# Seven products for eight on every superblock, with a new slot and mirror policy and all ReLUs on ScalarE: a gated-attention and maxout kernel

## The chip, the cores and the metric

One core of one Trainium2 chip runs the whole kernel in one launch. The metric is the device time of one execution in microseconds (us). Engine names: PE is TensorE's matmuls and PEld its weight loads, DVE is VectorE, ACT is ScalarE, POOL is GpSimd, SP is SyncE, which in this kernel only issues DMAs: four loads at the start, and from then on transposes. A suffix q (SPq, ACTq) marks work of an engine's sequencer, such as issuing a DMA.

The kernel before took 947.47 us (median of 3 runs, 943.57 to 948.69).

## The reference

```
B, S, D, d_qk, d_ff = 8, 3072, 256, 64, 1024
scores = z @ z^T / S                     # per batch, S x S, symmetric
x = u * (relu(scores)**2 @ v)            # gated attention, S x D
out = maximum(x @ w1, x @ w2) @ w_out    # maxout feed-forward, d_ff wide
```

The kernel uses max(a, b) = relu(a - b) + b, so the feed-forward becomes `relu(x @ (w1 - w2)) @ w_out + x @ (w2 @ w_out)`.

## The kernel before

A batch's 3072 rows are six groups of 512, and two groups make a superblock, so there are three superblocks per batch (c = 0, 1, 2) and 24 "couples" (batch, superblock). The squared scores are kept as blocks of 512 x 512 in bf16 slots of SBUF. Because scores are symmetric, only blocks on or above the diagonal are computed. The block below is the *mirror*, made by a DMA transpose. On a diagonal block three *triangle* pieces are mirrored. SyncE also issues the *turns*: transposes of u (for the gate) and of z (for the next scores).

From batch 1 on, a couple's attention product is not done as eight quarter products but as seven (P1, P5, P6, P7, X11, X12, X21), for which VectorE makes block sums S1 to S4 and sums of v. Before, this was done for the two superblocks off the diagonal (`o != c`), while the superblock's own blocks went plainly (D22 and the own parts of the X products). A couple is then:

- a *product stage*: 88 steps of two half-array matmuls, with the score pairs of later couples between them;
- two *ffs* of the couple before, during which VectorE works off a task list: gates of the couple just finished, then S1, S2, S3 and the sums of v for the next.

```python
def score_pair(b, g, m, ...):              # two score tiles: matmul, ReLU, square
    ...
    def finish():
        nc.vector.tensor_mul(a[:, k : k + 2, :], r, r)          # square (cut)
        if triangle and k:
            for j in range(G - 1):                              # 3 triangle pieces
                nc.sync.dma_start_transpose(a[:, j + 1 :, ts(j, P)], a[:, j, (j + 1) * P :])
        if k and blk > g:
            ...
            to_mirror.append((b, g, blk))
            mirror_ready()

def mirror_ready(keep=0):
    while to_mirror and len(free) > keep:  # mirror as soon as a slot is free
        mirror(*to_mirror.pop(0))

def turn_u(b, g):
    t = upool.tile([P, G, KD, P], bf16, name="uT")
    nc.sync.dma_start_transpose(t.rearrange(...), un[b, g].rearrange(...))

def ff(b, g, xT, ...):
    for nb in range(KF):                   # KF = 8 tiles d_ps
        ...                                # two matmuls into d_ps
        if nb in (2, 5, 7):
            nc.vector.tensor_single_scalar(out=g_sb[:, nb, :], in_=d_ps, scalar=0.0, op=ALU.max)
        else:
            nc.scalar.activation(g_sb[:, nb, :], d_ps, AF.Relu)
        hook(1, nb)                        # one VectorE task, at some places
    for t0 in range(0, G, 2):
        ...                                # 20 matmuls into o_ps
        nc.scalar.copy(o_sb, o_ps)
        nc.scalar.dma_start(out=dst[:, ds(t0, 2), :], in_=o_sb)   # the store: ScalarE issues it

# main loop, one couple (much cut)
(42 if b else 6, lambda: turn_u(b, q1)),   # program steps at which u is turned
(48 if b else 14, lambda: turn_u(b, q2)),
...
return forms, list(gates) + sums[:3] + tasks + sums[3:]   # VectorE's list: the gates come first
```

VectorE works its list in order, and the gates, which read the turned u, stand at its head: in the trace of before, gates, sums and sums of v run in the order of the list in all 21 couples that have sums. And the DMAs issued by SyncE and by ScalarE share eight completion semaphores: in before as in after, their 415 DMAs use eight in one common rotation, and in none of the 407 cases with a predecessor on the same semaphore does an issue start before that one has landed (the earliest starts 0.06 us after it in before, 0.08 in after). So a store on ScalarE may have to wait for a transpose that stands eight DMAs before it in the program; in after such waits held ScalarE's next copy 7 times, 60.2 us in all.

## Time and profile before

| | before |
|---|---|
| median of 3 runs | 947.47 us |
| span of the profiled run | 943.4 us |
| PE / DVE / ACT busy | 99% / 76% / 59% |
| product stage, medians of superblock 0 / 1 / 2 | 21.80 / 21.48 / 22.12 us |
| first ff / second ff | 8.04 / 8.09 to 8.14 us |

The stage times here and below are worked out from the timeline, as differences of the starts of matmul groups (first product matmul, first `d_ps` matmul of each ff), as medians over batches 1 to 6.

From the page of the profile of before: the span, the busy time of each engine with its share and instruction count, PE's busy tenths in 40 equal slices, and the shares of the chain of waits.

```profile
span 943.4 us, 19492 instructions
...
PE 929.3 (99%) x7706; PEld 517.5 (55%) x7706; DVE 717.3 (76%) x1158; ACT 552.8 (59%) x1062; POOL 57.0 (6%) x111
...
PE   8997999999999999999999999999999999999998
...
PE 91%; DVE 5%; ACT 1%; issue 1%; DMA 1%; SPq 0%; ACTq 0%; DVEq 0%
```

PE works in nearly every slice, and the chain that ended last is 91% PE. So here time is won only by removing matmuls and lost only by making PE wait.

Groups of before (line, engine, operation, tiles, count | busy us, mean ns of one | idle before, and what ended most of it):

```profile
L829 PE MATMUL acc<-blk,v_sb 64*128 64x512 bf16 x2544 | 467.1, 376 | 0.0
...
L829 PE MATMUL acc<-blk,vt 64*128 64x512 bf16 x1344 | 328.6, 376 | 0.0
...
L432 ACT ACTIVATE g_sb<-d_ps 128x512 bf16<-128x512 f32 x240 | 130.3, 599 | 56.8 <-PE d_ps L420 52.3
...
L428 DVE TENSOR_SCALAR g_sb<-d_ps 128x512 bf16<-128x512 f32 x144 | 96.2, 685 | 42.6 <-PE d_ps L420 34.2
```

The two L829 groups are the product matmuls, 3888 in all. The ffs' ReLUs are shared: 240 on ACT, 144 on DVE.

Waits of before by engine (us in total, times, longest):

```profile
PE d_ps L420 <- ACT o_sb L456: 3.9, 1, 3.9
...
PEld L448 <- DVE g_sb L428: 7.0, 21, 0.5
...
ACT o_sb L456 <- DMA blk<-blk: 6.1, 1, 6.1
```

PE hardly waits.

ScalarE's timeline of before at the end of a first ff:

```profile
389.82 0.34 ACTq L457 DMA_DIRECT2D out_dram<-o_sb  x1
390.26 2.74 ACT L432 ACTIVATE g_sb<-d_ps 128x512 bf16<-128x512 f32 x5 [0.47 <-PE d_ps L420]
```

The store of the last output tile is issued at once (the copy before it had ended at 389.79), and the second ff's ReLUs follow 0.1 us later.

### The profile page before, as it was taken

What the parts mean: (1) busy time and instruction counts of PE and PEld (TensorE: products, weight loads), DVE (VectorE), ACT (ScalarE), POOL (GpSimd) and SP (SyncE); (2) the same over time, 40 slices, a digit from 0 to 9 for tenths busy, and PEclk for the clock granted to TensorE, in tenths of its full rate; (3) what the DMA queues carried; (4) which work ended last, traced back from release to release, by engine and by line L of the source; (5) the groups of instructions that cost most, each with busy time, mean ns of one, the idle gap of its engine ahead of it and who ended that gap; (6) DMA issues with size and microseconds to landing.
All of it is one profiled execution on the core that took longest, in us unless ns stands there. A gap on an engine that the chain in (4) does not pass through costs nothing.

```text
span 943.4 us, 19492 instructions
## 1 busy us (share of the span) xinstructions
PE 929.3 (99%) x7706; PEld 517.5 (55%) x7706; DVE 717.3 (76%) x1158; ACT 552.8 (59%) x1062; POOL 57.0 (6%) x111
## 2 busy tenths in 40 slices
PE   8997999999999999999999999999999999999998
PEld 4454465554555555555546555465465554655555
DVE  6772588778887787987878869788688787885651
ACT  6793856556556566566565565655756657563333
POOL 3100000000000000000000000000000000000000
PEclk9998999999999999999999999999999999999999
DMA  9999999989999995998979999799979889985301
GB/s 190 148 201 210 164 209 157 133 162 186 148 166 143 159 205 119 174 160 159 185 127 157 164 173 182 119 180 151 172 165 134 172 158 174 153 156 106 80 24 67
DMA packets 388652, 146.00 MB, mean 155 GB/s; under 512 B 361936, under 2 KB 365904, under 8 KB 388560
## 3 DMA queue, kind: packets, MB, share of 16 engines
q1 hardware_dynamic: 359328, 90.09, 60.4%
q0 software_dynamic: 15408, 29.50, 20.6%
q10 hardware_dynamic: 13824, 25.17, 8.1%
q8 instruction: 60, 0.98, 0.5%
q14 instruction: 32, 0.26, 0.1%
HBM read 59.77 MB, written 25.17 MB: 90 GB/s over the span
## 4 chain that ended last, share of the span: by engine, by line
PE 91%; DVE 5%; ACT 1%; issue 1%; DMA 1%; SPq 0%; ACTq 0%; DVEq 0%
PE acc L829 44%; PE o_ps L448 16%; PE d_ps L420 15%; PE s_ps L201 7%; PE o_ps L440 4%; PE acc L259 4%; DVE xT L404 1%; DVE g_sb L428 1%; ACT r_sb L214 1%; DMA blk<-blk 1%; DVE h_sb L735 1%; DVE blk L311 1%; DVE blk L303 0%; DVE blk L307 0%; DVE blk L222 0%
## 5 line engine op out<-in xcount | busy, mean ns | idle before, releaser
L829 PE MATMUL acc<-blk,v_sb 64*128 64x512 bf16 x2544 | 467.1, 376 | 0.0
L214 ACT ACTIVATE r_sb<-s_ps 128x512 bf16<-128x512 f32 (+3 forms) x664 | 333.5, 554 | 127.3 <-PE s_ps L201 126.4
L829 PE MATMUL acc<-blk,vt 64*128 64x512 bf16 x1344 | 328.6, 376 | 0.0
L829 PEld LDWEIGHTS <-v_sb 64*128 64x128 bf16 x2544 | 183.7, 94 | 141.5 <-issue 4.6
L222 DVE TENSOR_TENSOR blk<-r_sb 128x1024 bf16<-128x1024 bf16 x251 | 171.1, 689 | 99.5 <-ACT r_sb L214 98.1
L448 PE MATMUL o_ps<-w_out_sb,g_sb 128*128 128x256 bf16 x1536 | 202.9, 273 | 1.2 <-DVE g_sb L428 0.4
L420 PE MATMUL d_ps<-xT,w_sb 128*128 128x512 bf16 x768 | 180.3, 382 | 5.2 <-ACT o_sb L456 3.9
L448 PEld LDWEIGHTS <-g_sb 128*128 128x128 bf16 x1536 | 150.0, 98 | 26.7 <-DVE g_sb L428 7.0
L829 PEld LDWEIGHTS <-vt 64*128 64x128 bf16 x1344 | 125.6, 94 | 70.7
L456 ACT COPY o_sb<-o_ps 128x512 f32<-128x512 f32 x96 | 56.3, 586 | 184.2 <-PE o_ps L448 174.5
L432 ACT ACTIVATE g_sb<-d_ps 128x512 bf16<-128x512 f32 x240 | 130.3, 599 | 56.8 <-PE d_ps L420 52.3
L420 PEld LDWEIGHTS <-w_sb 128*128 128x128 bf16 x768 | 73.4, 98 | 100.7 <-issue 24.7
L428 DVE TENSOR_SCALAR g_sb<-d_ps 128x512 bf16<-128x512 f32 x144 | 96.2, 685 | 42.6 <-PE d_ps L420 34.2
L201 PE MATMUL s_ps<-zT 64*128 64x512 bf16 (+3 forms) x672 | 124.1, 357 | 1.0 <-ACT zT L119 0.5
L735 DVE TENSOR_TENSOR h_sb<-h_sb,acc 128x512 f32<-128x512 f32 x147 | 96.9, 682 | 28.1 <-PE acc L829 27.4
L220 DVE TENSOR_TENSOR blk<-r_sb 128x512 bf16<-128x512 bf16 (+3 forms) x170 | 50.9, 324 | 41.8 <-ACT r_sb L214 40.7
L440 PE MATMUL o_ps<-W2o_sb,xT 128*128 128x256 bf16 x384 | 73.4, 273 | 0.0
L404 DVE SCALAR_TENSOR_TENSOR xT<-h_sb,uT 128x512 bf16<-128x512 f32 x96 | 63.3, 681 | 0.0
L201 PEld LDWEIGHTS <-zT 64*128 64x128 bf16 x672 | 35.1, 94 | 38.5 <-ACT zT L119 1.0
L259 PE MATMUL acc<-blk,v_sb 64*128 64x512 bf16 x384 | 50.6, 376 | 1.8 <-DVE blk L222 1.3
L311 DVE TENSOR_TENSOR blk<-blk,blk 128x2048 bf16<-128x2048 bf16 x42 | 51.4, 1223 | 1.2
L754 DVE TENSOR_TENSOR blk<-blk,blk 128x2048 bf16<-128x2048 bf16 x42 | 51.1, 1218 | 0.0
(53 smaller groups left out, 348.6 us busy)
## 6 DMA issues: line engine op xcount, KB each, us to landing
out_dram<-o_sb ACTq DMA_DIRECT2D x96, 256.0 KB, 2.8
un<-in_u_dram POOLq DMA_DIRECT2D x48, 256.0 KB, 6.8
v_sb<-in_v_dram POOLq DMA_DIRECT2D x21, 512.0 KB, 7.3
blk<-blk SPq DMA_TRANSPOSE x246, 5.5
zn<-in_z_dram POOLq DMA_DIRECT2D x21, 128.0 KB, 4.5
v_sb<-in_v_dram POOLq DMA_DIRECT2D x6, 256.0 KB, 7.1
blk<-in_moe_w_dram POOLq DMA_DIRECT2D x2, 512.0 KB, 6.2
uT<-un SPq DMA_TRANSPOSE x48, 3.4
```

The lines of the kernel that those rows point to most:

```text
L201: nc.tensor.matmul(s_ps[h][:, lo[h] :], zT[rows, z_at(b, blk * G + tiles[h]), :], zT[rows, q + lo[h] // P : q + G, :].rearrange("p t c -> ...
L214: nc.scalar.activation(o, s, AF.Relu)
L222: nc.vector.tensor_mul(a[:, k : k + 2, :], r, r)
L259: nc.tensor.matmul(a.out(acc[half, dc]), v_at(b, t, dc)[rows], a.moving(rows, j), start=first, stop=last,)
L404: lambda dc=dc: nc.vector.scalar_tensor_tensor(out=x[:, dc, :].rearrange("p (t r) -> p t r", r=P), in0=hs[dc].rearrange("p (t r) -> p t r" ...
L420: nc.tensor.matmul(d_ps, w15_sb[:, kc, ts(nb, P)], xT[:, kc, :], start=(kc == 0), stop=(kc == KD - 1),)
L428: nc.vector.tensor_single_scalar(out=g_sb[:, nb, :], in_=d_ps, scalar=0.0, op=ALU.max)
L432: nc.scalar.activation(g_sb[:, nb, :], d_ps, AF.Relu)
L440: nc.tensor.matmul(o_ps[:, t, :], xT[:, dc, ts(t0 + t, P)], W2o_sb[:, dc, :], start=(dc == 0), stop=False,)
L448: nc.tensor.matmul(o_ps[:, t, :], g_sb[:, nb, ts(t0 + t, P)], w_out_sb[:, nb, :], start=False, stop=(nb == KF - 1),)
L735: nc.vector.tensor_add(out, a, b_)
L829: mm = nc.tensor.matmul(a.out(acc[name]), w()[rows], a.moving(rows, j), start=name not in opened, stop=left[name] == 0,)
```

## The change

The intent: use the seven products for the own superblock too, which saves 4 of 88 steps per couple. The extra sums load VectorE, so the ffs' ReLUs all go to ScalarE. The extra blocks need slots, so the slots' use is rearranged: 28 slots (T1, one of the sums of v, is written in v's own place, and there are four h buffers, which hold partial results, in place of five), a slot that a DMA transpose has read rests 40 steps before it is taken again, and mirrors with even g + blk are postponed until enough slots are free or until the couple that needs them is prepared.

```diff
-    NSLOTS = 27
+    NSLOTS = 28
+    KEEP = 5, 2
+    COOL = 40
@@ release: a slot read by a transpose rests
-                free.append(self.ap)
+                free.append((self.ap, tick + after))
@@ the mirror policy
-    def mirror_ready(keep=0):
-        while to_mirror and len(free) > keep:
-            mirror(*to_mirror.pop(0))
+    def urgent(b, g, blk):
+        return b == 0 or (g + blk) % 2
+
+    def mirror_ready(now=None, keep=0):
+        for only in (True, False):
+            for x in list(to_mirror):
+                if urgent(*x) if only else (x[0], x[1] // 2) == now:
+                    if at_hand() > (0 if only else keep):
+                        to_mirror.remove(x)
+                        mirror(*x)
@@ prepare: the own superblock gets S1, S2, S3 as well
-        for o in range(NC):
-            if o == c:
-                continue
+        for o in (c, *(o for o in range(NC) if o != c)):
@@ products: no D22, no own parts
-        (("P1", "P6", "P7", "X11"), ("X11", "P1", "P6", "P7")),
-        (("D22", "X12", "P5", "X21"), ("P5", "X21", "D22", "X12")),
+        (("P1", "P7", "P6", "X11"), ("P6", "X11", "P1", "P7")),
+        (("X21", "X12", "P5"), ("P5", "X12b", "X21")),
@@ ff: every ReLU on ScalarE
-            if nb in (2, 5, 7):
-                nc.vector.tensor_single_scalar(
-                    out=g_sb[:, nb, :], in_=d_ps, scalar=0.0, op=ALU.max
-                )
-            else:
-                nc.scalar.activation(g_sb[:, nb, :], d_ps, AF.Relu)
+            nc.scalar.activation(g_sb[:, nb, :], d_ps, AF.Relu)
@@ prepared: mirrors still missing are forced here; S3 comes last
+            for x in list(to_mirror):
+                if x[0] == b and x[2] // 2 == c:
+                    to_mirror.remove(x)
+                    mirror(*x)
-            return forms, list(gates) + sums[:3] + tasks + sums[3:]
+            first, *others = [x[:2] for x in sums]
+            tasks = list(gates) + first + tasks + sum(others, [])
+            return forms, tasks + [x[2] for x in sums]
@@ main loop: score pairs may be held back for want of a slot
-                mirror_ready()
-                for _ in at_step.get(s, ()):
+                mirror_ready((b, c), KEEP[s > 36])
+                asked += len(at_step.get(s, ()))
+                while asked and len(due) < 3 and (
+                    at_hand() or pairs[done][2] % 2 or len(steps) - s < 8 * asked
+                ):
                     emit_pair(wait=6)
+                    asked -= 1
# cut: the layouts of mixed sums, the new places of the P, X and S4 events
```

More of the change, by code (lines that the diff above doesn't have):

```diff
@@ L55 @@
     rpool = ctx.enter_context(tc.tile_pool(name="rpool", bufs=3))
-    hpool = ctx.enter_context(tc.tile_pool(name="hpool", bufs=5))
+    hpool = ctx.enter_context(tc.tile_pool(name="hpool", bufs=4))
     xpool = ctx.enter_context(tc.tile_pool(name="xpool", bufs=4))
@@ L64, in by_tile, with at_hand @@
         return x.rearrange("(p t) d -> p t d", t=NT)
-    free = [apool.tile([P, G * GW], bf16, name=f"blk{n}") for n in range(NSLOTS)]
+    free = [(apool.tile([P, G * GW], bf16, name=f"blk{n}"), 0) for n in range(NSLOTS)]
+    tick = 0
+    def at_hand():
+        return sum(ready <= tick for ap, ready in free)
     class Block:
         def __init__(self, turned=False, uses=1):
-            self.ap = free.pop(0)
+            best = min(range(len(free)), key=lambda n: max(free[n][1], tick))
+            self.ap = free.pop(best)[0]
             self.turned = turned
@@ L83, in out, with release @@
             return acc.rearrange("p (k r) -> p k r", r=P) if self.turned else acc
-        def release(self):
+        def release(self, after=0):
             self.uses -= 1
             if not self.uses:
-                free.append(self.ap)
+                free.append((self.ap, tick + after))
     zT = zpool.tile([P, 4 * 2 * G, P], bf16, name="zT", bufs=1)
@@ L157, in combine_v @@
         b21, b22 = w[:, G : 2 * G, 0:P], w[:, G : 2 * G, P:D]
-        t = tpool.tile([P, 4, G, P], bf16, name="vt")
-        vt[b, piece] = t
+        t = tpool.tile([P, 3, G, P], bf16, name="vt")
+        t1, t2, t3, t4 = vt[b, piece] = b12, t[:, 0], t[:, 1], t[:, 2]
         return [
-            lambda: nc.vector.tensor_sub(t[:, 0], b12, b11),
-            lambda: nc.vector.tensor_sub(t[:, 2], b22, b12),
-            lambda: nc.vector.tensor_sub(t[:, 1], b22, t[:, 0]),
-            lambda: nc.vector.tensor_sub(t[:, 3], b21, t[:, 1]),
+            lambda: nc.vector.tensor_sub(t3, b22, b12),
+            lambda: nc.vector.tensor_sub(t1, b12, b11),
+            lambda: nc.vector.tensor_sub(t2, b22, t1),
+            lambda: nc.vector.tensor_sub(t4, b21, t2),
         ]
@@ L246, in mirror @@
         A[b, blk, g] = t
-        A[b, g, blk].release()
+        A[b, g, blk].release(after=COOL)
     def acc_tile(n):
@@ L285, in drain_fast, with alike @@
         return hs
+    def alike(*blocks):
+        if len({x.turned for x in blocks}) == 1:
+            return [x.ap for x in blocks]
+        return [
+            x.ap.rearrange("p (k j r) -> p j k r", k=G, r=P)
+            if x.turned
+            else x.ap.rearrange("p (j k r) -> p j k r", k=G, r=P)
+            for x in blocks
+        ]
     def prepare(b, c):
         forms, tasks = {}, []
-        for o in range(NC):
-            if o == c:
-                continue
+        for o in (c, *(o for o in range(NC) if o != c)):
             f = {
@@ L301, in s1, with s2 @@
             def s1(f=f):
-                f["S1"] = Block(f["A21"].turned)
-                nc.vector.tensor_add(f["S1"].ap, f["A21"].ap, f["A22"].ap)
+                f["S1"] = Block(f["A22"].turned)
+                nc.vector.tensor_add(*alike(f["S1"], f["A21"], f["A22"]))
+            def s2(f=f):
+                f["S2"] = Block(f["A22"].turned)
+                nc.vector.tensor_sub(*alike(f["S2"], f["S1"], f["A11"]))
             def s3(f=f):
                 f["S3"] = f["A21"]
-                nc.vector.tensor_sub(f["S3"].ap, f["A11"].ap, f["A21"].ap)
-            def s2(f=f):
-                f["S2"] = Block(f["A21"].turned)
-                nc.vector.tensor_sub(f["S2"].ap, f["S1"].ap, f["A11"].ap)
-            tasks += [s1, s2, s3]
+                nc.vector.tensor_sub(*alike(f["S3"], f["A11"], f["A21"]))
+            tasks.append([s1, s2, s3])
         return forms, tasks
     ORDER = (
-        (("P1", "P6", "P7", "X11"), ("X11", "P1", "P6", "P7")),
-        (("D22", "X12", "P5", "X21"), ("P5", "X21", "D22", "X12")),
+        (("P1", "P7", "P6", "X11"), ("P6", "X11", "P1", "P7")),
+        (("X21", "X12", "P5"), ("P5", "X12b", "X21")),
     )
-    BANK = {"P1": 0, "P6": 1, "P7": 2, "X11": 3, "D22": 0, "P5": 1, "X21": 2, "X12": 3}
+    BANK = {"P1": 0, "P6": 1, "P7": 2, "X11": 3, "X21": 0, "P5": 1, "X12": 2, "X12b": 3}
     PLAIN_BANK = {"D11": 0, "D12": 1, "D21": 2, "D22": 3}
-    OFF = {
+    FORM = {
         "P1": ("A11", 11),
@@ L329 @@
         "X12": ("S4", 22),
+        "X12b": ("S4", 22),
     }
-    OWN = {"X11": (0, 0), "X12": (0, 1), "X21": (1, 0), "D22": (1, 1)}
     def product(b, c, forms, name):
-        off, own = [], []
-        if name in OFF:
-            form, side = OFF[name]
-            for o in forms:
-                for j in range(G):
-                    if side >= 10:
-                        k, dc = side // 10 - 1, side % 10 - 1
-                        w = lambda o=o, j=j, k=k, dc=dc: v_at(b, (2 * o + k) * G + j, dc)
-                    else:
-                        w = lambda o=o, j=j, side=side: vt[b, o][:, side, j, :]
-                    off.append((name, w, lambda o=o, form=form: forms[o][form], j))
-        if name in OWN:
-            q, dc = OWN[name]
-            for k in range(2):
-                for j in range(G):
-                    own.append((
-                        name,
-                        lambda k=k, j=j, dc=dc: v_at(b, (2 * c + k) * G + j, dc),
-                        lambda k=k, q=q: A[b, 2 * c + q, 2 * c + k],
-                        j,
-                    ))
-        return own + off if name in ("X12", "X21") else off + own
+        form, side = FORM[name]
+        steps = []
+        for o in forms:
+            for j in range(G):
+                if side >= 10:
+                    k, dc = side // 10 - 1, side % 10 - 1
+                    w = lambda o=o, j=j, k=k, dc=dc: v_at(b, (2 * o + k) * G + j, dc)
+                else:
+                    w = lambda o=o, j=j, side=side: vt[b, o][side][:, j, :]
+                steps.append((name, w, lambda o=o, form=form: forms[o][form], j))
+        return steps
     PLAIN_LANES = (("D11", "D12", "D21", "D22"), ("D21", "D22", "D11", "D12"))
@@ L426, in ff @@
                 )
-            if nb in (2, 5, 7):
-                nc.vector.tensor_single_scalar(
-                    out=g_sb[:, nb, :], in_=d_ps, scalar=0.0, op=ALU.max
-                )
-            else:
-                nc.scalar.activation(g_sb[:, nb, :], d_ps, AF.Relu)
+            nc.scalar.activation(g_sb[:, nb, :], d_ps, AF.Relu)
             hook(1, nb)
@@ L488 @@
     due = []
-    tick = 0
     def emit_pair(wait=0):
@@ L589 @@
             for slot, (n, dc) in enumerate(steps_of(i)):
+                tick += 1
                 k = need(b, g, n)
@@ L678, in hook @@
                         tasks.pop(0)()
+            nonlocal tick
             for q in range(2):
@@ L682, in second @@
                 ff(b, g, xTs.pop((b, g)), hook=hook)
+                tick += 32
             while tasks:
@@ L698, in prepared @@
             for o in reversed(range(NC)):
-                if o != c and (b, o) not in vt:
+                if (b, o) not in vt:
                     tasks += combine_v(b, o)
             forms, sums = prepare(b, c)
-            return forms, list(gates) + sums[:3] + tasks + sums[3:]
+            first, *others = [x[:2] for x in sums]
+            tasks = list(gates) + first + tasks + sum(others, [])
+            return forms, tasks + [x[2] for x in sums]
         b, g = groups[PLAIN - 1]
@@ L726 @@
                     f[name].quota = 2 * G * n
-            for q in (q1, q2):
-                for k in (q1, q2) if b else range(NG):
-                    A[b, q, k].quota = 4 * G
+            if not b:
+                for q in (q1, q2):
+                    for k in range(NG):
+                        A[b, q, k].quota = 4 * G
             for pair in steps:
@@ L747, in after_p7 @@
                 add(h["U3"], h["U2"], acc["P7"])
-            def after_x11():
-                h["x"] = new_h()
-                nc.scalar.copy(h["x"], acc["X11"])
             def s4(f):
@@ L758, in c11, with after_p5 @@
             def c11():
-                add(h["1"], h["1"], h["x"])
-            def after_d22():
-                h["V"] = new_h()
-                add(h["V"], h["U3"], acc["D22"])
-            def after_p5():
-                add(h["V"], h["V"], acc["P5"])
-                add(h["U2"], h["U2"], acc["P5"])
+                add(h["1"], h["1"], acc["X11"])
             def after_x12():
                 add(h["U2"], h["U2"], acc["X12"])
+                add(h["U2"], h["U2"], acc["X12b"])
+            def after_p5():
+                h["V"] = new_h()
+                add(h["V"], h["U3"], acc["P5"])
+                add(h["U2"], h["U2"], acc["P5"])
             def after_x21():
                 add(h["U3"], h["U3"], acc["X21"])
-            f = list(forms.values())
-            events = {}
             def after_plain():
@@ L781, in after_plain @@
                     copy(h[name], acc[name])
+            events = {}
+            f = list(forms.values())
             for n, do in () if not b else (
-                (ends["P1"], after_p1),
+                (ends["P6"], after_p1),
                 (ends["P6"], after_p6),
-                (ends["P6"] + 2, lambda: s4(f[0])),
                 (ends["P7"], after_p7),
-                (ends["X11"], after_x11),
-                (ends["X11"] + 3, lambda: s4(f[1])),
-                (ends["X11"] + 7, c11),
-                (ends["D22"], after_d22),
+                (ends["X11"], c11),
+                (ends["X11"] - 7, lambda: s4(f[0])),
+                (ends["X11"] - 3, lambda: s4(f[1])),
+                (ends["X11"] + 1, lambda: s4(f[2])),
+                (ends["X12"], after_x12),
                 (ends["P5"], after_p5),
-                (ends["X12"], after_x12),
                 (ends["X21"], after_x21),
@@ L813 @@
                         events.setdefault(n, []).append(do)
+            asked = 0
             for s, pair in enumerate(steps):
@@ L846 @@
                         a.release()
+            assert not asked, (i, asked)
             flush()
```

## The prediction

> What bounds the kernel now. TensorE: the page gives PE 929.3 us of 943.4 (99%), and the chain of waits is 91% PE. The three-couple windows from 110 us on show 109.8 of 110 us PE at full clock, DVE about 89, ACT about 66. One couple lasts 38.0 us (first product-to-ff boundary at 343.0, the next at 381.0 in the chain): 21.9 us of products and score pairs, 16.1 us of two ffs. So only two things count: matmuls removed, and new waits of PE.
>
> Removed. A couple had 88 steps (3888 half-array matmuls on the product line / 21 / 2); with seven products for all three superblocks it has 7*3*4 = 84. A step takes 0.2155 us in the timeline. 21 * 4 * 0.2155 = 18.1 us less PE, all on the critical path. That is 1.9%, so even free of cost the change can hardly be faster by 2%.
>
> Moved and added, DVE. Per couple three more sums (S1, S2, S3) and one more S4, 128x2048 bf16 at 1.22 us each: +103 us in all. The 144 ff ReLUs leave DVE: -96 us (0.685 us each). DVE ends near 720 to 730 us, as before, provided the sums of mixed layouts keep 1.22 us. [...] I expect about 1.2 us.
>
> ACT. +144 ReLUs, -21 X11 copies: 553 + 86 - 12 = about 627 us busy, 66%. On average enough, but not within an ff. An ff issues eight d_ps tiles in 3.46 us (0.432 each), and its output matmuls reach the eighth g tile 4.45 us after the start. ACT's ReLUs back to back follow every 0.536 us (five in 2.74 us). First ff of a couple: ACT's first ReLU starts 0.65 us after the first d_ps matmul, so the eighth ends at 0.65 + 7*0.536 + 0.595 = 5.0 us; PE resumes near 5.07 instead of 4.67 today: +0.40 us. Second ff: ACT first copies the last o_ps of the first ff (0.59) and issues its store (0.34); its first ReLU starts at 1.26 us, the eighth ends at 5.6; PE resumes near 5.68 instead of 4.61: +1.07 us. [...] 24 couples * 1.47 = +35 us, all on the critical path.
>
> Slots, h, tpool. Two more slots live per couple against one more slot; the 40-step rest and postponed score pairs should avoid DVE standing behind a transpose. Bunched score pairs and the tighter bank handovers (12 steps, 2.6 us, for a ScalarE copy and a DVE add after P6) I put at +3 us in all.
>
> Sum: 947.5 - 18.1 + 35.3 + 3 = about 967 us, on the edge of 2% slower.
>
> What would show it. Product line 3528 matmuls. Product stage of a couple 21.1 us; ffs about 8.5 and 9.1 us. In the waits, the load of g_sb waiting for ACT g_sb: about 0.6 and 1.1 us per ff, 40 us in total; today only 7 us for DVE. ACT near 627, DVE near 725; PE busy share down to about 95%. No PE wait of length for blk.
>
> What would make it wrong. Lower: if ACT's ReLUs pipeline faster back to back, or the ff waits are filled: down to 930. Higher: late score pairs pushing ACT's backlog into the first ff; DVE held by a transpose through a hot slot; [...] P6 or P7 banks freed late.

The sum: 947.5 - 18.1 + 35.3 + 3 = 967.7, the 3 being a guess of mine. That the mixed sums keep about 1.2 us, and that nothing fills PE's gaps in the ffs, were assumptions of mine.

## More of the kernel before

SyncE's timeline of before in the product stage of a couple of superblock 1 (397.09 to 418.6 us; start, duration, what it issued), up to the turns of u:

```profile
398.61 2.61 SPq L133 DMA_TRANSPOSE zT<-zd  x2
401.33 2.28 SPq L243 DMA_TRANSPOSE blk<-blk  x1
403.72 8.79 SPq L225 DMA_TRANSPOSE blk<-blk  x6
412.61 2.63 SPq L177 DMA_TRANSPOSE uT<-un  x2
```

The two turns of u are issued together 15.5 us into the stage, directly behind the six triangle pieces, and so are done before the stage ends. Issuing one transpose occupied SyncE for 1.12 to 8.95 us in before (median 1.49 of 315).

## The result and the profile after

The kernel after took 1028.94 us (median of 4 runs, 1024.76 to 1036.31), against 948.08 (4 runs, 943.57 to 955.7) for the kernel before on the same chip: a ratio of 1.0852, 95% interval 1.0758 to 1.0947. Executions over 1.5% slower than the fastest of the same kernel are left out of the means. A ratio here is the mean time of one kernel's fast runs over the mean of the other's fast runs of the same rounds, so it is not quite the ratio of the medians quoted. The prediction was about 967 us: the measured median is 62 us above it.

From the page of the profile of after, the same lines as of before:

```profile
span 1034.5 us, 19244 instructions
...
PE 946.3 (91%) x7538; PEld 515.4 (50%) x7538; DVE 718.3 (69%) x1098; ACT 604.1 (58%) x1185; POOL 57.1 (6%) x111
...
PE   9998999969998799978999789987999969998998
...
PE 51%; DVE 15%; DMA 14%; ACT 11%; issue 4%; SPq 3%; ACTq 1%; DVEq 0%
```

PE is busy 91% instead of 99%, and the slices show dips at regular distances: something recurs once per batch. PE's busy time is even higher than before (946.3 us against 929.3), though there are 168 matmuls fewer; part of the reason is given below with the clock. In the chain, DVE, DMA and ACT now hold 40% together. DVE's busy time is what it was (718 us), and ACT's is 604 us: no engine is short of time on average.

```profile
L842 PE MATMUL acc<-blk,v_sb 64*128 64x512 bf16 x2208 | 455.3, 377 | 0.0
...
L842 PE MATMUL acc<-blk,vt 64*128 64x512 bf16 x1512 | 369.3, 377 | 6.6 <-DVE blk L329 5.7
...
L438 ACT ACTIVATE g_sb<-d_ps 128x512 bf16<-128x512 f32 x384 | 195.4, 626 | 54.2 <-PE d_ps L431 41.1
...
L329 DVE TENSOR_TENSOR blk<-blk,blk 128x2048 bf16<-128x2048 bf16 x63 | 77.2, 1225 | 2.1
```

The matmuls were saved as intended: 3720 product matmuls, 168 fewer. All 384 ReLUs are on ACT. The block sums, some of which now mix two layouts, keep 1.22 us (L329: 1225 ns). The waits:

```profile
PE d_ps L431 <- ACT o_sb L462: 44.7, 7, 7.8
PE d_ps L431 <- ACT g_sb L438: 12.8, 7, 3.4
...
PEld L454 <- ACT g_sb L438: 20.7, 61, 0.4
...
ACT o_sb L462 <- DMA blk<-blk: 60.2, 7, 10.0
...
DVE xT L415 <- DMA uT<-un: 113.9, 19, 10.6
```

Read from the bottom: VectorE stood 113.9 us, 19 times, before a gate, waiting for a turn of u. ScalarE stood 60.2 us, 7 times, on a block's transpose (before: once, 6.1). PE stood 44.7 us, 7 times, before `d_ps`, for the bank that ScalarE's copy of `o_ps` frees, and 12.8 us more for ScalarE's ReLUs. Only the wait of PEld on `g_sb`, 20.7 us, is one I had predicted (as 40).

Where in time: the stage table says which couples. Mean total of a couple, and medians of its parts, batches 1 to 6:

| superblock | before: stage / ff / ff / total | after: stage / ff / ff / total |
|---|---|---|
| 0 | 21.80 / 8.04 / 8.09 / 37.94 | 20.94 / 8.11 / 8.77 / 38.59 |
| 1 | 21.48 / 8.04 / 8.14 / 37.67 | 23.16 / 8.11 / 19.81 / 51.24 |
| 2 | 22.12 / 8.04 / 8.09 / 38.26 | 21.26 / 8.11 / 8.77 / 38.15 |

Every batch loses its time in the same place, the couple of superblock 1: its product stage (a wait of up to 2.4 us for turned z about the middle, in some batches waits for S2 near the start), and above all the second ff. An undisturbed couple of after gains 0.86 us in the product stage (4 steps of 0.2155) and loses 0.07 + 0.68 us in the ffs, so it is worth 0.11 us. In the profiled run the six disturbed couples took 51.15, 50.63, 50.38, 51.57, 52.18 and 51.54 us. Undisturbed they would take 37.50 (20.62 + 8.11 + 8.77, the 20.62 from run e1_turn_early below), so their holes are 82.4 us. Batch 1's first couple took 42.38 instead of 37.83, and the last batch's superblock 1 40.76 instead of the 36.10 of e1_turn_early. That makes 91.6. 1034.5 - 91.6 = 942.9, against 943.4 before: by this sum over the profiled run, **the holes are the whole of the slowdown, and without them the change would be worth nothing**.

One such couple, product stage from 301.37 to 324.07 us, second ff from 332.2 us. First SyncE's timeline of after, to compare with the lines of before:

```profile
307.56 2.79 SPq L140 DMA_TRANSPOSE zT<-zd  x2
310.45 5.57 SPq L257 DMA_TRANSPOSE blk<-blk  x1
316.12 8.34 SPq L232 DMA_TRANSPOSE blk<-blk  x6
324.56 1.78 SPq L257 DMA_TRANSPOSE blk<-blk  x1
326.76 1.52 SPq L184 DMA_TRANSPOSE uT<-un  x1
328.39 2.55 SPq L257 DMA_TRANSPOSE blk<-blk  x1
331.03 1.29 SPq L184 DMA_TRANSPOSE uT<-un  x1
332.42 4.46 SPq L257 DMA_TRANSPOSE blk<-blk  x1
```

The turns of u (L184) are issued 25.4 and 29.7 us after the stage's start, after its end, because postponed mirrors (L257) stand before and between them. In the program's order, one batch of transposes on SyncE reads (M mirror, t triangle piece, U turn of u, Z turn of z, the second pair of U is superblock 1's): before `tttttt UU MMMM ZZ M tttttt UU M tttttt M Z MMM UU MMMMM`, after `tttttt M U MM U MM ZZ M tttttt M U M U M tttttt M Z M UU MMMM`. VectorE in the same couple, and then ScalarE and PE:

```profile
336.88 1.29 DVE L415 SCALAR_TENSOR_TENSOR xT<-h_sb,uT 128x512 bf16<-128x512 f32 x2 [5.07 <-DMA uT<-un]
338.09 1.22 DVE L325 TENSOR_TENSOR blk<-blk,blk 128x2048 bf16<-128x2048 bf16 x1
```

```profile
324.71 4.03 ACT L438 ACTIVATE g_sb<-d_ps 128x512 bf16<-128x512 f32 x8 [0.75 <-PE d_ps L431]
330.20 0.58 ACT L462 COPY o_sb<-o_ps 128x512 f32<-128x512 f32 x1 [1.47 <-PE o_ps L454]
338.69 0.34 ACTq L463 DMA_DIRECT2D out_dram<-o_sb  x1
339.13 0.58 ACT L462 COPY o_sb<-o_ps 128x512 f32<-128x512 f32 x1 [8.34 <-DMA blk<-blk]
342.21 0.34 ACTq L463 DMA_DIRECT2D out_dram<-o_sb  x1
342.59 1.57 ACT L438 ACTIVATE g_sb<-d_ps 128x512 bf16<-128x512 f32 x3 [2.88 <-DMA blk<-blk]
```

```profile
339.77 1.01 PE L431 MATMUL d_ps<-xT,w_sb 128*128 128x512 bf16 x2 [6.12 <-ACT o_sb L462]
343.24 3.15 PE L431 MATMUL d_ps<-xT,w_sb 128*128 128x512 bf16 x7 [2.46 <-ACT g_sb L438]
```

Four steps:

1. The second turn of u, issued at 331.03, lands 5.8 us later, and the second pair of gates starts at 336.88 after 5.07 us of waiting. Only then may VectorE begin S1 (L325, 338.09).
2. ScalarE copied the first half of an output by 330.78, but issues its store only at 338.69. Its semaphore belonged to the mirror issued at 332.42, which landed 6.2 us later, at 338.62. The second store at 342.21 waits likewise, for the triangle piece issued at 336.97, which landed at 342.13.
3. In the trace ScalarE keeps the program's order: in all 48 ffs its records read eight ReLUs, copy, store, copy, store. So the copies and ReLUs behind the stores stand too; the ReLUs at 342.59 start 0.04 us after the store's issue at 342.21 has ended.
4. PE writes three `d_ps` tiles from 332.19 on and has then no bank free: four banks serve `d_ps` and `o_ps`, and the fourth holds the output that ScalarE has not copied. PE stands 6.12 us, writes one tile, and stands 2.46 us more.

PE's granted clock is 0.965 in this run. The trace shows where it is lost: in each of the six holes of batches 1 to 6 it is 0.5 for 10.24 us (in the couple above from 338.3 to 348.5), and each time PE had then been standing for 3.6 to 4.7 us. In batches 1 to 6 of before it never dips. So the dip comes after the wait has begun and is not its cause. But it adds to the loss: the second ff above is 11.0 us longer than an undisturbed one, its two waits are 8.6 us, and in the other 2.5 us PE works at half clock (eight output matmuls from 347.03 on take 1.59 us, the next eight 0.87). This slow work counts as busy (six of those eight matmuls are recorded at 421 ns, the next eight at 272 to 273).

### The profile page after: what moved, and what is told of

The parts are those of the page before. It is cut to its first block, busy times and chain, and to the rows that moved or that the text cites. A ratio compares the mean times of both kernels' runs of the same rounds, so it can differ in the third digit from the quotient of the medians.

```text
span 1034.5 us, 19244 instructions
## 1 busy us (share of the span) xinstructions
PE 946.3 (91%) x7538; PEld 515.4 (50%) x7538; DVE 718.3 (69%) x1098; ACT 604.1 (58%) x1185; POOL 57.1 (6%) x111
## 4 chain that ended last, share of the span: by engine, by line
PE 51%; DVE 15%; DMA 14%; ACT 11%; issue 4%; SPq 3%; ACTq 1%; DVEq 0%
PE acc L842 28%; ACT g_sb L438 10%; PE o_ps L454 9%; DMA uT<-un 7%; PE s_ps L208 5%; DMA blk<-blk 4%; PE acc L273 4%; PE d_ps L431 3%; SPq L257 3%; DMA zT<-zd 3%; DVE blk L229 3%; DVE h_sb L750 3%; DVE blk L325 2%; DVE blk L333 2%; PE o_ps L446 2%
## 5 line engine op out<-in xcount | busy, mean ns | idle before, releaser
L842 PE MATMUL acc<-blk,v_sb 64*128 64x512 bf16 x2208 | 455.3, 377 | 0.0
L842 PE MATMUL acc<-blk,vt 64*128 64x512 bf16 x1512 | 369.3, 377 | 6.6 <-DVE blk L329 5.7
L842 PEld LDWEIGHTS <-v_sb 64*128 64x128 bf16 x2208 | 175.3, 94 | 151.4 <-issue 23.2
L431 PE MATMUL d_ps<-xT,w_sb 128*128 128x512 bf16 x768 | 195.7, 400 | 57.5 <-ACT o_sb L462 44.7
L438 ACT ACTIVATE g_sb<-d_ps 128x512 bf16<-128x512 f32 x384 | 195.4, 626 | 54.2 <-PE d_ps L431 41.1
L454 PE MATMUL o_ps<-w_out_sb,g_sb 128*128 128x256 bf16 x1536 | 211.9, 276 | 6.5 <-ACT g_sb L438 4.1
L454 PEld LDWEIGHTS <-g_sb 128*128 128x128 bf16 x1536 | 151.9, 99 | 39.4 <-ACT g_sb L438 20.7
L842 PEld LDWEIGHTS <-vt 64*128 64x128 bf16 x1512 | 139.2, 94 | 64.3 <-issue 0.5
L415 DVE SCALAR_TENSOR_TENSOR xT<-h_sb,uT 128x512 bf16<-128x512 f32 x96 | 61.1, 685 | 113.9 <-DMA uT<-un 113.9
L750 DVE TENSOR_TENSOR h_sb<-h_sb,acc 128x512 f32<-128x512 f32 x168 | 109.3, 681 | 43.0 <-ACT h_sb L754 35.5
L765 DVE TENSOR_TENSOR blk<-blk,blk 128x2048 bf16<-128x2048 bf16 x63 | 76.6, 1218 | 5.6 <-PE acc L842 5.6
L329 DVE TENSOR_TENSOR blk<-blk,blk 128x2048 bf16<-128x2048 bf16 x63 | 77.2, 1225 | 2.1
L325 DVE TENSOR_TENSOR blk<-blk,blk 128x2048 bf16<-128x2048 bf16 x63 | 76.7, 1218 | 2.4 <-DMA blk<-blk 2.4
L333 DVE TENSOR_TENSOR blk<-blk,blk 128x2048 bf16<-128x2048 bf16 x63 | 73.3, 1218 | 0.0
L227 DVE TENSOR_TENSOR blk<-r_sb 128x512 bf16<-128x512 bf16 (+3 forms) x170 | 45.0, 319 | 33.2 <-ACT r_sb L221 33.0
```

What stands on the lines that cost most here:

```text
L325: nc.vector.tensor_add(*alike(f["S1"], f["A21"], f["A22"]))
L329: nc.vector.tensor_sub(*alike(f["S2"], f["S1"], f["A11"]))
L333: nc.vector.tensor_sub(*alike(f["S3"], f["A11"], f["A21"]))
L431: nc.tensor.matmul(d_ps, w15_sb[:, kc, ts(nb, P)], xT[:, kc, :], start=(kc == 0), stop=(kc == KD - 1),)
L454: nc.tensor.matmul(o_ps[:, t, :], g_sb[:, nb, ts(t0 + t, P)], w_out_sb[:, nb, :], start=False, stop=(nb == KF - 1),)
L750: nc.vector.tensor_add(out, a, b_)
```

## The experiments

The theories. **A**: the order on SyncE's queue; postponed mirrors push the turns of u, and with them VectorE and the stores, behind the end of the stage. **B**: ScalarE's load; with all ReLUs and no slack it falls behind and PE waits for it. **C**: the 40-step rest and the lack of free slots. All runs were correct against the reference. "Before" is the kernel before in the same rounds on the same chip: 947.56 us for e1 to e4, 945.72 for e5 to e8, 946.66 for e9 to e12, 945.14 for e13 to e18.

### e1_turn_early: the turns of u moved forward

```diff
-                (42 if b else 6, lambda: turn_u(b, q1)),
-                (48 if b else 14, lambda: turn_u(b, q2)),
+                (34 if b else 6, lambda: turn_u(b, q1)),
+                (35 if b else 14, lambda: turn_u(b, q2)),
```

> The changed kernel with one edit: the two turns of u are issued at steps 34 and 35 of the product stage instead of 42 and 48, so that they stand ahead of the mirrors in SyncE's queue and side by side. Theory A (queue order: the second turn of u stands behind mirrors, the gates on VectorE wait for it, VectorE holds back the next transposes, the stores' completion counters hold ScalarE, TensorE stops in the second ff): the twelve-microsecond hole of every third couple goes, VectorE's wait for uT falls from 114 us to under 25, time 945 to 965 us. Rival B (the ReLUs on ScalarE make the loss) and rival C (too few slots, whatever the order): stays above 1010 us.

Measured: 993.45 us (984.04 to 998.0), ratio 1.0458 [1.0382, 1.0534]. Between the two expectations. The waits of this kernel:

```profile
PE d_ps L431 <- ACT o_sb L462: 34.2, 7, 6.0
...
ACT o_sb L462 <- DMA blk<-blk: 49.7, 7, 8.2
...
DVE blk L325 <- DMA blk<-blk: 47.5, 19, 4.4
```

The gates no longer wait at all, and 36 us are back. But SyncE's queue is as long as before: now S1 waits for a mirror (47.5 us, 19 times) and the stores still wait for transposes. The second ff of superblock 1 takes 15.51 us instead of 19.81. So the late turn was not quite half of the story.

### e2_before_relu_act: the kernel before, with all ReLUs on ScalarE

```diff
-            if nb in (2, 5, 7):
-                nc.vector.tensor_single_scalar(...)
-            else:
-                nc.scalar.activation(g_sb[:, nb, :], d_ps, AF.Relu)
+            nc.scalar.activation(g_sb[:, nb, :], d_ps, AF.Relu)
```

> The kernel before with one edit: all eight ReLUs of ff on ScalarE. The prediction's sum says +35 us (982). The trace of the changed kernel shows ffs of 8.11 and 8.77 us in its undisturbed couples against 8.04 and 8.09 before, which gives 24*0.75 = +18 us (966). Rival B (the ReLUs make the whole loss): 1020 or more.

Measured: 970.13 us (963.63 to 975.7), ratio 1.0222 [1.0148, 1.0296]. The ffs become 8.11 and 8.77 us, exactly as in after: +0.75 us per couple, 18 us for 24 couples. The other 4.6 us I put down to holes, which the unprofiled runs can't show: the profiled run, the second slowest at 973.68 us, has one of 7.7 us. So the ReLU part of the change costs 22.6 us by itself (1.5% to 3.0%), and its regular part is the same in both kernels. It does not bring the holes of after.

### e3_after_cool0: after, without the 40-step rest

```diff
-    COOL = 40
+    COOL = 0
```

> The changed kernel with COOL = 0: a slot freed by a DMA turn may be taken at once. Rival C (the rest of 40 steps starves the slots and so delays mirrors): below 1000 us. Theory A: SyncE's order of transposes is nearly the same, so 1015 to 1050 us, if anything longer because VectorE now stands behind transposes that still read the slot it is to write (a wait of DVE for DMA blk of over 10 us in total).

Measured: 1037.72 us (1035.0 to 1045.99), ratio 1.0938 [1.0875, 1.1001]. Not faster: the squares on VectorE now stand behind transposes that still read the slot (65.1 us for one form and 45.0 for the other, neither among the large waits of after). The 40-step rest does what it was made for, and C falls as far as the rest goes; whether slots are too few for the mirrors to come earlier is tested by e5.

### e4_before_policy: the kernel before, with the new slot and mirror policy alone

The edit is the change's slot list with the rest, `urgent`, the new `mirror_ready`, the forced mirrors and the held-back pairs, on the old 88 steps with 27 slots, five h and the old ReLUs.

> The kernel before (88 steps, ReLUs shared, 27 slots, five h) with only the changed slot and mirror policy (rest of 40 steps, urgent mirrors first, held-back score pairs). Its two turns of u stay side by side in SyncE's queue, behind at most two mirrors more than before. Theory A: 945 to 970 us. Rival D (the policy alone loses the time, with any products): above 1000 us.

Measured: 978.11 us (969.08 to 980.64), ratio 1.0292 [1.0222, 1.0362], more than I expected. Superblock 1's couple is 41.64 us instead of 37.67, and gates wait for turns (16.7 us, 9 times). So the policy alone, without a single new product or ReLU, makes holes in the same couple, only shallower. They come by another link: most of the loss is in the first ff (10.92 us, the second 9.32), where PE waits mainly for the ReLUs on VectorE (14.4 us, 9 times), which stand behind the waiting gates.

### e5_eager: after, with no mirror postponed

```diff
     def urgent(b, g, blk):
-        return b == 0 or (g + blk) % 2
+        return True
```

> The changed kernel with one edit: every mirror counts as urgent, so it is turned as soon as a rested slot is at hand, as the kernel before did. SyncE's order becomes the one before (both turns of u side by side, no mirror between or right ahead of them, three fewer mirrors left for the end of the second superblock of a batch). Theory A' (what costs is the mirrors postponed into the stretch where the turns of u and the twelve triangle transposes stand): 945 to 970 us, waits of DVE for uT under 30 us, holes in the second ff under 3 us. Rival C (too few slots for the seven products): mirrors do not come earlier, time stays above 1000.

Measured: 969.73 us (966.18 to 976.59), ratio 1.0257 [1.0177, 1.0338]. One line gives back 59 us of the 81, within the expected range. The order of transposes on SyncE is then the same as before's, letter by letter, so the 28 slots were enough for early mirrors, and C falls here altogether. No gate waits for a turn any more, and superblock 1's couple falls from 51.24 to 39.75 us; one hole of its second ffs is still 3.3 us, a little over the 3 expected.

### e6_early_eager: e1 and e5 together

> E1 and E5 together: turns of u at steps 34 and 35 and every mirror urgent. Theory A': at least as fast as either alone, 938 to 955 us; the sum of the stages of an undisturbed batch in E1 (38.15 + 37.83 + 37.5) times seven plus the start and end would be 938. Rival (the two cures are the same thing and a third wait stays): no better than E5.

Measured: 957.57 us (955.63 to 962.38), ratio 1.0127 [1.0072, 1.0182]. That is 2.6 us above the expected range. Of the 81 us, 71 are gone. SyncE in the stage of a superblock 1 that starts at 636.43 us:

```profile
649.04 2.65 SPq L184 DMA_TRANSPOSE uT<-un  x2
```

The turns are issued 12.6 us into the stage (after: 25.4 and 29.7), and superblock 1's couples take 38.94 us in the mean. A is right as far as the cause of the holes goes, once it includes the mirrors' own lateness and not only the turns'.

### e7_stores_on_pool: after, with the stores issued by GpSimd

```diff
-            nc.scalar.dma_start(out=dst[:, ds(t0, 2), :], in_=o_sb)
+            nc.gpsimd.dma_start(out=dst[:, ds(t0, 2), :], in_=o_sb)
```

> The changed kernel with one edit: ff's output stores are issued from GpSimd instead of ScalarE, so that no late transpose can hold ScalarE through a store's completion counter. If the held ScalarE is the only link from the late transposes to TensorE: 945 to 965 us. If the sums on VectorE are late all the same (gates wait for uT): the hole moves from the second ff to the start of the next product stage and the time stays above 1000 us.

Measured: 1007.35 us (1004.35 to 1021.97; the highest run was slow, and the median of the three fast ones is 1005.5), ratio of the fast runs 1.0635 [1.0571, 1.0698]. If the stores on ScalarE are the link between the transposes and PE, taking them away must end PE's wait in the second ff. It did: the second ff takes 8.27 us in all three superblocks (8.05 by the records, in which a first matmul of the second ff is missing and moves the boundary by 0.22 us). But the backlog came out at the next link:

```profile
PE s_ps L208 <- DMA zT<-zd: 34.5, 11, 6.6
PE acc L842 <- DVE blk L329: 10.8, 9, 2.0
...
DVE xT L415 <- DMA uT<-un: 89.9, 19, 6.4
```

The gates still wait for turns, VectorE is still late, and now PE waits in the product stage of superblock 2 (28.69 us instead of 21.26) for turned z and for S2. So the stores are how the delay reaches PE first, not where it comes from.

### e8_early_pool: e1 with the stores on GpSimd

> E1 with the stores on GpSimd. In E1 what is left is 7 us in the second ff of every third couple, where ScalarE's store is released by a landing mirror. If that is all: 940 to 950 us. If the sums behind the mirrors (DVE blk waits for DMA blk, 47 us in E1) stop TensorE next: 965 to 990 us, with the hole at the start of the product stage.

Measured: 1008.72 us in its one fast run; three of four runs and the profile were slow (1027.42 to 1032.6), and there is no ratio. Nothing is read from it.

### e9_after_relu_shared: after, with the ReLUs 2, 5 and 7 back on VectorE

```diff
-            nc.scalar.activation(g_sb[:, nb, :], d_ps, AF.Relu)
+            if nb in (2, 5, 7):
+                nc.vector.tensor_single_scalar(
+                    out=g_sb[:, nb, :], in_=d_ps, scalar=0.0, op=ALU.max
+                )
+            else:
+                nc.scalar.activation(g_sb[:, nb, :], d_ps, AF.Relu)
```

> The changed kernel with ff's ReLUs 2, 5 and 7 given back to VectorE, as before; nothing else. If the ReLUs on ScalarE made the loss, 950 or less. Theory A' (mirrors postponed to the end of the stage) has the holes stay: 1010 to 1060 us; ffs of undisturbed couples back to about 8.1 us each, but VectorE 96 us busier and later.

Measured: 1063.92 us (1058.82 to 1069.0), ratio 1.1224 [1.1145, 1.1304]. That is just above the 1010 to 1060 expected. B falls as the cause of the holes (its own share is that of e2), and the opposite is true: relieving ScalarE makes it worse by 35 us, because VectorE then has 809 us of work and its list gets late.

```profile
PE 950.2 (89%) x7490; PEld 523.7 (49%) x7538; DVE 809.2 (76%) x1242; ACT 540.6 (51%) x1041; POOL 57.0 (5%) x111
```

In its waits, PE stands 43.1 us on VectorE's ReLUs and 19.2 us in the products on S2 (in after 5.7).

### e10_early_eager_relu_shared and e11_balanced: e6 with ReLUs on VectorE

e10 is e6 with the edit of e9. e11 moves only two of eight, at places chosen so that they do not meet VectorE's list, and moves two S4 by 5 steps:

```diff
+            if nb in ((2, 5) if g % 2 else (4, 6)):
+                nc.vector.tensor_single_scalar(...)
...
-            places = {(1, 0): 1, (1, 3): 1, (2, 0): 1, (2, 1): 1, (2, 2): 1, (2, 3): 1}
+            places = {(1, 6): 1, (2, 0): 1, (2, 1): 1, (2, 2): 1, (2, 3): 1}   # first ff only
...
-                (ends["X11"] - 3, lambda: s4(f[1])),
-                (ends["X11"] + 1, lambda: s4(f[2])),
+                (ends["X11"] + 2, lambda: s4(f[1])),
+                (ends["X11"] + 6, lambda: s4(f[2])),
```

> E6 (turns of u early, every mirror urgent) with ReLUs 2, 5 and 7 back on VectorE: the seven products with none of the three schedule changes that were found costly. If VectorE could carry sums and ReLUs both, 940 us (E6 less 24*0.75). If it can't (718+96 = 814 us busy, 34+4 of about 37.5 us a couple), the S2 sums come late and the product stage waits at its start: 955 to 985 us.

> E6 with two ReLUs of eight on VectorE, placed where it is free (4 and 6 in a couple's first ff, with the gates after them, 2 and 5 in the second), and two S4 sums moved 5 steps later so that P7's bank is drained in time. Product stages 20.6 to 21.3 us, ffs about 8.0 and 8.2: 930 to 945 us. If VectorE is too full, S2 sums are late and the time is 950 or more.

Measured: e10 1044.04 us (1040.85 to 1047.64), ratio 1.1016 [1.0944, 1.1087], DVE 806 us busy. e11 1010.15 us (1000.5 to 1013.22), ratio 1.0668 [1.0587, 1.0749], DVE 780 us. With e6's 719 us at 957.57, time rises with VectorE's load: 61 us more of it cost 53 us, and 87 us more cost 86, though VectorE is idle over a fifth of the span in all three. The couples of superblock 0 and 1 pay for it in the stage or the second ff (e11: 25.97 us for superblock 0's stage, about 13 for superblock 1's second ff). In e11, 11.6 us of PE's waits are for the S4 that I had moved, so part of its cost is that edit's own. e10 missed both branches of its expectation; e11 fell in its second, "950 or more". VectorE was my blind spot: busy shares of 75 to 78% look harmless, but its list in the two ffs is full.

### e12_before_policy_eager: e4, with no mirror postponed

The edit is that of e5, on e4's kernel.

> E4 (the kernel before with the changed slot policy, 978 us) with every mirror urgent: what is left of the policy is the rest of 40 steps and the held-back score pairs. Theory A': its 31 us come from the postponed mirrors, so 945 to 957 us here. Rival: the rest itself costs, 965 to 985 us.

Measured: 948.88 us (945.78 to 954.09), ratio 1.0016 [0.9947, 1.0085]: the kernel before again. So in the old products too, the postponed mirrors are the whole cost of the policy (29 us), and the rest, the held-back pairs and the choice of slots cost nothing that these runs can tell (the interval is -0.5% to +0.9%).

### e13 to e15: what is left of e6

e6 still stands 12 us above before. Its stage table shows three terms: the second ff 8.77 us (8.56 by the records, with a first matmul missing as in e7; before 8.09), the stages of superblocks 0 and 1 at 21.82 and 21.71 us, which is all of their gain lost again (undisturbed 20.94 and 20.62), and single waits in superblock 1. In these stages PE waits for VectorE's add that frees P7's bank (2.9 us in the list of its waits, 13 times), since the score pairs now keep VectorE busy there. e13_store_later issues the first ff's last store after the fourth ReLU of the second ff. e14_p7_on_act lets ScalarE copy P7's bank, so that the bank is free before VectorE has come to it. e15_both does both.

```diff
# e13_store_later
+            if nb == 3 and held_store:
+                held_store.pop()()
...
-            nc.scalar.dma_start(out=dst[:, ds(t0, 2), :], in_=o_sb)
+            if g % 2 == 0 and t0 == 2:
+                held_store.append(store)
+            else:
+                store()
# e14_p7_on_act
                 h["U3"] = new_h()
-                add(h["U3"], h["U2"], acc["P7"])
+                nc.scalar.copy(h["U3"], acc["P7"])
+                events.setdefault(ends["P7"] + 4, []).append(
+                    lambda: add(h["U3"], h["U3"], h["U2"])
+                )
```

> E6 with the last store of a couple's first ff issued by ScalarE after the fourth ReLU of the second ff. If the store's 0.34 us lag costs what it takes: second ff 0.3 us shorter, 24*0.3 = 7 us, so 950 us. If ScalarE then only waits elsewhere: 957.

> E6 with P7's bank copied out by ScalarE at the end of P7 and added to U2 by VectorE four steps later. If the bank is what stops the product stage at its 60th step: stages of the first two superblocks 0.4 to 0.6 us shorter, 14 couples, 950 us. If not: 957, or more for ScalarE's extra 12 us.

> The edits of E13 and E14 together on E6: 943 us if both act, 950 us if only one of the two does, 957 us if neither.

Measured: e13 951.63 us (950.26 to 958.86), ratio 1.0094 [1.0047, 1.0141]; the second ff falls to 8.26. e14 959.17 us (953.69 to 966.46), ratio 1.0158 [1.0102, 1.0214]; the stages fall to 21.24 and 21.12, but this gain is hidden by single holes (in its profile a second ff of batch 0 takes 21.14 us, against 13.38 in e6's). e15 942.01 us (938.15 to 952.15), ratio 0.9988 [0.9928, 1.0048]: level with before. The page of e15:

```profile
PE 919.2 (98%) x7538; PEld 524.5 (56%) x7538; DVE 717.8 (76%) x1098; ACT 598.6 (64%) x1206; POOL 57.1 (6%) x111
```

PE is busy 98% of a span that is 4 us shorter than before's.

### e16_all, e17_triangles_spread, e18_both_again: can it be beaten?

e16 is e15 with ReLU 2 on VectorE for superblocks 0 and 2's second ffs; e17 is e15 with four score pairs fewer in superblock 1's stage, so that fewer triangle pieces meet the turns there; e18 is e15 once more, with more rounds.

```diff
# e16_all
-            nc.scalar.activation(g_sb[:, nb, :], d_ps, AF.Relu)
+            if nb == 2 and g in (1, 5):
+                nc.vector.tensor_single_scalar(out=g_sb[:, nb, :], in_=d_ps, scalar=0.0, op=ALU.max)
+            else:
+                nc.scalar.activation(g_sb[:, nb, :], d_ps, AF.Relu)
# e17_triangles_spread
-            target = min((b + 1) * per_batch + (-6, 8, 22)[c], len(pairs))
+            target = min((b + 1) * per_batch + (-6, 4, 22)[c], len(pairs))
```

> E15 with the third ReLU of the second ff on VectorE in superblocks 0 and 2, whose ffs run beside few sums. If ScalarE's pace is the tail: 16 * 0.45 = 7 us less than E15, 936 us. If VectorE's 11 us more work counts as in E11: 945 or more.

> E15 with the score pairs of one diagonal block (three triangle transposes) moved from superblock 1's stage to superblock 2's. If the remaining hole is the backlog of transposes in superblock 1: second ffs of superblock 1 at 8.26 us in all batches, runs alike, 936 to 941 us and a ratio under 0.995. If it is something else, or ScalarE is too full with 18 score pairs in one stage: 942 us or more.

> E15 unchanged, five rounds on the chip that runs E17: 938 to 945 us in most runs, ratio to the kernel before 0.993 to 1.000.

Measured: e16 944.51 us (940.51 to 952.88), ratio 1.0009 [0.9953, 1.0066]; in its profile superblock 1's mean couple is 40.06 us against 38.09 in e15's. The 10 us more on VectorE (727 against 718) could be the reason, but this isn't shown: e18's profile, of e15's own kernel, has 39.87. e17 945.69 us (940.8 to 953.41), ratio 1.0021 [0.9977, 1.0064]; in its profile superblock 1 has no hole in any batch, but the last stage of batch 0 has one of 8.1 us. Nor are the moved pairs free: superblock 1's stage is 1.20 us shorter than in e15 and superblock 2's 1.92 us longer. e18 945.49 us (940.23 to 954.02), ratio 1.0003 [0.9959, 1.0047]; only two of its six runs lie in the 938 to 945 us that I expected of most. None of them beats the kernel before. e15's runs lie from 938 to 952, and only the profiled ones can be read: e15's, at 941.14, has one wait of ScalarE's copy on a block's transpose (5.9 us), and e18's, at 954.02, has four, 23.6 us in all.

## Why the prediction was wrong, point by point

**What bounds the kernel: right.** PE, and only matmuls removed and new waits of PE count. The difference is PE's waiting, and the half clock (0.5 for 10.24 us) measured in each of the six long holes.

**The matmuls removed, -18.1 us: right.** 168 fewer, and each product stage that is undisturbed is 0.86 us shorter: 21 x 0.86 = 18.1. (The count that I gave for the product line, 3528, forgot the 192 plain ones of batch 0's last couple; it is 3720.)

**VectorE, 720 to 730 us and mixed sums at 1.22 us: right.** 718.3 us and 1218 to 1225 ns in the mean, against 1218 to 1223 in before; of the 252 block sums of after, the mixed ones among them, none took over 1226 ns.

**ScalarE's ReLUs, "24 couples * 1.47 = +35 us": right in mechanism, twice too large.** I took 0.536 us per ReLU from a run of five in before. On ScalarE alone, eight take 4.03 us, 0.49 us from start to start ((4.03 - 0.6) / 7). So the ffs lost 0.07 and 0.68 us instead of 0.40 and 1.07: 24 x 0.75 = 18 us. ACT's busy time came out at 604 instead of 627 us for the same reason: its 384 ReLUs were busy for 195.4 us, where my sum had 130.3 + 86.

**"Slots, h, tpool ... +3 us in all" and "No PE wait of length for blk": this is the step that failed.** Word for word the second nearly holds (PE waited 5.7 us for a block sum), because the blocks' transposes reached PE by way of VectorE and ScalarE. The term of +3 us measured 59 us for the postponed mirrors alone (e5 against after; 29 us on the old products, e12 against e4), 71 with the turns moved too (e6), and 92 us of holes in the profiled run, all of them of PE. (The three are not the same sum: e5 and e6 are differences of medians, the last counts what the profiled run loses in every hole.) I had read the policy as something that spares VectorE, which it is (e3), and had not drawn SyncE's queue in program order. Had I written down the letters M, t, U and Z, the turns between forced mirrors would have been visible without a run. The wait of before, ACT's 6.1 us on a block's transpose, was in the profile, and I passed it over. In my list of what could go wrong stood "late score pairs pushing ACT's backlog into the first ff" and "DVE held by a transpose through a hot slot". Neither is it (in after VectorE waited 2.4 us in all for a block's transpose, and e12 shows the held-back pairs free on the old products): VectorE was held by a turn in the queue behind mirrors, and ScalarE by its stores' semaphores.

So the sum should have read -18.1 + 18 + 81, the last being what is left of the measured difference, for the new waits. With no holes the change is worth nothing, and e15, with few holes, ties: it takes back part of the ReLU term and keeps part of the products' gain (its stages of superblocks 0 and 1 are 21.24 and 21.12 us, undisturbed 20.94 and 20.62).

**What stays open.** First, why a single transpose's issue sometimes occupies SyncE for 4 to 6 us (5.57 at 310.45 above) while the next take 1.3. It is not a wait for another DMA's semaphore: in none of the 407 cases above does the record of an issue start before the DMA with its semaphore has landed, and the trace lists SyncE's waits for semaphores as records of their own (ahead of the mirrors of after, up to 13.5 us). The loads of u, v and z, which GpSimd issues, run at such times, and contention with them is my reading. The trace of after fits it: from 100 us on, a mirror's issue had a median of 2.16 us when none of GpSimd's loads was in flight at its start (66 mirrors), 3.21 with one (22), 6.07 with two (6) and 6.65 with three (10), and before's trace rises likewise (2.22, 3.79, 5.15, 7.19). That is a correlation; no run moved the loads. Second, the holes of superblock 1 that come and go between runs of e15, and the single 8 us hole in batch 0's stage in the profiles of e13 and e17. Third, why VectorE's load costs nearly as much as it adds (e10, e11): the order of its list would explain it, but I did not measure the slack at each place.

## What to carry to other kernels

Before postponing DMAs, write down the issuing engine's queue in program order and look at what is put behind the postponed ones: SyncE's queue, which only issues, had a length in us (in after, a turn of u occupied SyncE for a median of 1.71 us, 1.23 to 4.15, and landed 4.2 us after its issue began, 3.1 to 10.2; a mirror's issue had a median of 2.99 us, 1.32 to 10.75, and its landing 5.9), and here seven-eighths of the loss went when the same 319 DMAs of SyncE were put in another order (e6). Look also for an engine that both computes and issues DMAs: here ScalarE's copies stood for what its stores' issues waited for, 8.34 us before one copy, 60.2 us in all. And weigh a change's halves against each other first: a saving of 18 us that needs an 18 us move elsewhere has nothing to pay for any accident.
